# Block 1 of x through ACT's queue, the second gate weights moved ahead of blocks 2 and 3, and blocks 6 and 7 transposed by DMA

## The chip, the cores and the metric

The kernel runs on one core of a Trainium2 chip. The metric is the device time of one execution in microseconds (us); lower is better. The engines are named as in the profile: PE (TensorE, matmuls; PEld are its weight loads), DVE (VectorE), ACT (ScalarE), POOL (GpSimd) and SP (SyncE, which only issues DMAs here). PEq, ACTq and SPq are their instruction sequencers.

## The reference

The input x has 2048 tokens of 512 values. It is normalized, and two branches of the normalized x are added to x: a sliding-window attention (32 heads of 16, window 256) and a gated MLP whose gate is mixed over the tokens by a 2048 x 2048 matrix.

```python
xn = _layernorm(x)                                   # 2048 x 512
# branch A
q, k, v = split_heads(xn @ wqkv)                     # 32 heads of 16
p = softmax(where(0 <= i - j < 256, q @ k.T / 4, -1e9))
a = (p @ v) @ wo
# branch B
z = gelu(xn @ w_in)                                  # 2048 x 1376
z1, z2 = z[:, :688], _layernorm(z[:, 688:])
g = w_sp @ z2 + b_sp[:, None]                        # over the tokens
b = (z1 * g) @ w_out
out = x + a + b
```

All inputs and the output are bfloat16.

## The kernel before

The 2048 tokens are 16 blocks of 128 rows. The program is scheduled by hand: every engine runs its instructions in the order in which the code emits them, and a queue of DMAs goes out in the order of its issue.

The first stage (to about 54 us) makes the normalized and transposed x, called `xnT` (features on the partitions), and the two halves of z for each block. For a block n it consists of these steps:

- `load_x(n2)` (L189) loads blocks 2 n2 and 2 n2 + 1 into a tile `xs` by one DMA of 256 KB on SP's queue. With `split=True`, used for blocks 0 and 1 alone, it issues one DMA of 128 KB for each block (L194).
- `load_win(half, c0, c1)` (L203) loads two of the four row chunks of half of `w_in`, 344 KB. Half 1 gives z2 (the gate), half 0 gives z1.
- `stats(n)` (L252) computes mean and variance on DVE (L254, L255, L119) and the reciprocal root on POOL (L120).
- `norm(n)` (L258) normalizes on DVE (L260) into a tile `xn`. For n >= `X_DMA` (8) a DMA transpose on SP's queue then writes `xnT` (L265). For the others the tile is kept for `transpose_x(n)` (L269): four transposes on PE into PSUM (L274) and a copy by ACT (L277).
- `do_z(n, half)` (L279) runs eight matmuls on PE, four chunks by two column ranges (L285), and a GELU on ACT (L293).
- `z2_stats` and `z2_norm` normalize z2 on DVE (L298 to L304).

The order of DMAs on SP at the start is: block 0, block 1, gate weights chunks 0 and 1, blocks 2 and 3, gate weights chunks 2 and 3, blocks 4 and 5, the two parts of half 0 of `w_in`, blocks 6 and 7, `wqkv` (1536 KB), blocks 8 to 15, `wo`, and two pieces of `w_out`. Two one-element memsets on DVE hold some of them back: L313 (after the statistics of block 0) the half 0 of `w_in`, and L326 (after the statistics of block 3) `wqkv` and with it everything behind it on SP. After these come the DMA transposes of blocks 8 to 15 and of the first two rows of blocks of `w_sp` (`load_wsp`).

On PE the order is: 9 warm-up matmuls, transposes of block 0, 3 more warm-up matmuls, transposes of block 1, the gate half of blocks 0 and 1, transposes of block 2, half 0 of block 0, and then a loop over n from 2, whose body is

```python
            if n + 1 < X_DMA:
                transpose_x(n + 1)
            if n < NB:
                do_z(n, 1)
            if n + 3 < NB:
                stats(n + 3)
            if n + 2 < NB:
                norm(n + 2)
```

followed by `z2_stats(n - 2)`, the z2 norms, one of nine early projections of q, k or v once n >= 5 (`proj`, L129), and `do_z(n - 1, 0)`. ACT begins with the load of its function table and a warm-up activation (L216). A POOL instruction that forms a mask (L222) waits for this.

The second stage works through the list `ORDER`: scores, exponentials on ACT (L491), masks, values, the mixing of z2 with `w_sp` (L402) and the output (L433, L439, L444).

Of the kernel before, what the change touches and what calls it, by code (L numbers as in the profile page):

```python
# [8 lines left out]
P = 128  # L9
# [19 lines left out]
Z_RANGES = [(0, 512), (512, FH)]  # L29
NRING = 6  # L30
EBUFS = 7
X_DMA = 8
LAST = 128
ONB = 4
N_WARM = (9, 3)
# [33 lines left out]
def kernel(  # L69
# [12 lines left out]
    nc = tc.nc  # L82
    x2 = A_x.flatten_outer_dims()
# [94 lines left out]
    with tc.tile_pool(name="win_pool", bufs=1) as winp, tc.tile_pool(  # L178
# [10 lines left out]
        def load_x(n2, split=False):  # L189
            xs = xsp.tile([P, 2, D], BF, name="xs")  # L190
            if split:
                for j in range(2):
                    r = (2 * n2 + j) * P
                    nc.sync.dma_start(out=xs[:, j, :], in_=x2[r : r + P, :])  # L194
            else:
                nc.sync.dma_start(  # L196
                    out=xs[:],
                    in_=x2[2 * n2 * P : (2 * n2 + 2) * P, :].rearrange("(j p) d -> p j d", p=P),
                )
            for j in range(2):  # L200
                xs_tiles[2 * n2 + j] = xs[:, j, :]

        def load_win(half, c0, c1):  # L203
            nc.sync.dma_start(
                out=w_in_sb[:, c0:c1, half * FH : (half + 1) * FH],
                in_=B_w_in[c0 * P : c1 * P, half * FH : (half + 1) * FH].rearrange(
                    "(c p) f -> p c f", p=P
                ),
            )

        load_x(0, split=True)
        load_win(1, 0, 2)
        load_x(1)
        load_win(1, 2, 4)
        warm = sml.tile([P, 1], F32, name="warm")
        nc.scalar.activation(out=warm[:], in_=esel[:, 0:1], func=ACT.Gelu_apprx_tanh)  # L216

# [1 line left out]
            out=fmask[:], in_=fmask[:], pattern=[[-1, P]], compare_op=ALU.is_gt,  # L219
# [3 lines left out]
            out=esel[:], in_=esel[:], pattern=[[-32, 4]], compare_op=ALU.is_ge,  # L223
# [3 lines left out]
            out=esel[:], in_=esel[:], pattern=[[32, 4]], compare_op=ALU.is_ge,  # L227
# [30 lines left out]
        def norm(n):  # L258
# [4 lines left out]
            )  # L263
            if n >= X_DMA:
                nc.sync.dma_start_transpose(out=xnT[:, :, n * P : (n + 1) * P], in_=xn[:])  # L265
# [3 lines left out]
        def transpose_x(n):  # L269
            xn = xn_tiles.pop(n)  # L270
            pool, tag = (ps_y, "y") if n == 1 else (ps_g, "g")
            tp = pool.tile([P, NDC, P], BF, name="tp", tag=tag)
            for c in range(NDC):
                nc.tensor.transpose(  # L274
                    out=tp[:, c, :], in_=xn[:, c * P : (c + 1) * P], identity=ident[:]
                )
            nc.scalar.copy(out=xnT[:, :, n * P : (n + 1) * P], in_=tp[:])  # L277
# [34 lines left out]
        stats(0)  # L312
        nc.vector.memset(w_in_sb[0:1, 0, 0:1], 0.0)  # L313
        load_x(2)
        load_win(0, 0, 2)
        load_win(0, 2, 4)
# [12 lines left out]
        for n2 in range(4, NB // 2):  # L329
# [3 lines left out]
            out=w_out_sb[:, 0:5, :], in_=B_w_out[0:640, :].rearrange("(c p) n -> p c n", p=P)  # L333
# [9 lines left out]
            out=emask[:, 0:1], in_=esel[:], op=ALU.add, axis=mybir.AxisListType.X  # L343
        )
        nc.vector.tensor_scalar(
            out=emask[:, 1:2], in0=emask[:, 0:1], scalar1=-1.0, scalar2=1.0,
# [3 lines left out]
        for n in range(2, NB + 1):  # L350
            if n + 1 < X_DMA:
                transpose_x(n + 1)
# [220 lines left out]
    for i, t in enumerate(tokens):  # L573
        if i == last_proj + 1:
            for n in range(NB):
                xres[n] = xnT[:, n % NDC, (n // NDC) * D : (n // NDC + 1) * D]
            for c in range(NDC):
                nc.sync.dma_start(
                    out=xnT[:, c, :].rearrange("p (m d) -> p m d", d=D),
                    in_=x2.rearrange("(m c p) d -> c p m d", p=P, c=NDC)[c],  # L580
# [46 lines left out]
```

## Time and profile before

| | |
|---|---|
| median of 3 runs | 268.03 us (267.9 to 268.32) |
| the profiled execution's own time | 268.1 us |
| its span, first to last instruction | 266.1 us |
| TensorE clock granted | 1.0 throughout |
| PE busy | 258.6 us |
| ACT busy | 206.0 us |
| DVE busy | 197.3 us |
| POOL busy | 123.6 us |
| DMA | 23.63 MB, mean 89 GB/s |

The page has the busy time of each engine, a chain of waits followed back from the last instruction, and the costliest groups of instructions. The trace behind it can be asked for the order in time of a stretch (timeline: start, length, engine, line, operation; in brackets the idle time of the engine before it and what ended that), for the pieces of the chain in order of time, for the DMAs (KB of each and the us from issue to landing, a median where there are several) and for the busy time of each engine in given stretches. All times are from the start of the span. A DMA's time to landing holds its wait behind DMAs issued before it. The chain counts a pipelined matmul from the end of the one before it, so a piece of it can begin up to 0.2 us after the instruction's own start in the timeline.

### The profile page before, as it was taken

Reading aid. Unit: us, or ns where it says so; the run is one execution under the profiler, and the core shown is the slowest. Engines: PE = TensorE matmul, PEld = TensorE weight load, DVE = VectorE, ACT = ScalarE, POOL = GpSimd, SP = SyncE. Lnnn points to the kernel's source line nnn. Section 1 sums busy time; section 2 is a strip of 40 time slices with the busy share of each in tenths; the row PEclk is TensorE's granted clock in tenths of the full one; section 3 lists DMA queues with packets and bytes.
Section 4 is the critical chain, followed back from the end, with each engine's and each line's share of the span. In section 5 each row is a group of like instructions: output and inputs, shape, how many; then the busy total and the mean of one; then the engine's idle time right before and its main releaser. Section 6 shows DMA issues by size and latency. Waiting matters only on the chain.

```text
span 266.1 us, 8418 instructions
## 1 busy us (share of the span) xinstructions
PE 258.6 (97%) x3661; PEld 147.1 (55%) x3694; DVE 197.3 (74%) x384; ACT 206.0 (77%) x235; POOL 123.6 (46%) x140
## 2 busy tenths in 40 slices
PE   7999999999999999999999999999999999999995
PEld 2565665645455547554656656655665454554543
DVE  5999999567766778968788888767777658568542
ACT  3677767699999999999999899897899789553000
POOL 4334454115645256746637493156573617247200
PEclk9999999999999999999999999999999999999999
DMA  6992325700504050251312054033059972423733
GB/s 204 350 363 55 61 40 112 88 2 2 110 15 98 2 111 21 63 46 38 81 31 52 17 66 81 2 81 83 15 130 272 143 123 59 98 74 30 150 91 89
DMA packets 60132, 23.63 MB, mean 89 GB/s; under 512 B 51216, under 2 KB 59584, under 8 KB 60096
## 3 DMA queue, kind: packets, MB, share of 16 engines
q1 hardware_dynamic: 59472, 22.70, 38.5%
q8 instruction: 29, 0.48, 0.7%
q10 hardware_dynamic: 576, 0.39, 0.5%
q0 software_dynamic: 48, 0.00, 0.3%
q14 instruction: 7, 0.06, 0.1%
HBM read 8.41 MB, written 2.10 MB: 39 GB/s over the span
## 4 chain that ended last, share of the span: by engine, by line
PE 88%; ACT 7%; DMA 2%; issue 1%; SPq 1%; DVE 0%; ACTq 0%
PE gf L402 28%; PE zs L285 14%; PE S L483 11%; PE m L151 8%; PE o_t L531 8%; PE fo L439 8%; ACT E L491 7%; PE m L135 5%; PE fo L433 5%; DMA w_in_sb<-in_B_w_in_dram 2%; PE tp L274 1%; ACT L491 0%; DVE xnT L444 0%; SPq L194 0%; SPq L196 0%
## 5 line engine op out<-in xcount | busy, mean ns | idle before, releaser
L491 ACT ACTIVATE E<-S 128x1024 bf16<-128x1024 f32 x180 | 168.4, 1056 | 18.1 <-PE S L483 14.1
L402 PE MATMUL gf<-z_all,wspT 128*128 128x344 bf16 x512 | 94.2, 310 | 0.0
L502 POOL TENSOR_SCALAR_AFFINE_SELECT E<-E 128x1024 bf16<-128x1024 bf16 x64 | 79.3, 1264 | 18.1 <-ACT E L491 18.0
L402 PEld LDWEIGHTS <-wspT 128*128 128x128 bf16 x512 | 44.2, 98 | 33.8 <-issue 10.5
L554 POOL TENSOR_TENSOR o_norm<-o_c,rsum 128x256 bf16<-128x256 f32 x32 | 23.2, 726 | 77.3 <-DVE rsum L552 77.3
L507 DVE TENSOR_TENSOR E<-E,fmask 128x1024 bf16<-128x1024 bf16 x56 | 51.9, 954 | 1.6 <-ACT E L491 1.5
L285 PE MATMUL zs<-w_in_sb,xnT 128*128 128x176 bf16 (+1 forms) x250 | 39.7, 307 | 0.7 <-DMA w_in_sb<-in_B_w_in_dram 0.4
L483 PE MATMUL S<-q,k 32*128 32x128 bf16 (+2 forms) x888 | 38.5, 251 | 0.8 <-ACT E L491 0.8
L293 ACT ACTIVATE z_all<-zs 128x688 bf16<-128x688 f32 x32 | 23.8, 744 | 12.5 <-PE zs L285 12.5
L151 PE MATMUL m<-xnT,wqkv 128*128 128x512 bf16 x110 | 31.3, 379 | 0.9
L285 PEld LDWEIGHTS <-xnT 128*128 128x128 bf16 x256 | 22.2, 98 | 15.3 <-issue 0.6
L409 DVE SCALAR_TENSOR_TENSOR z_all<-gf,b_all,z_all 128x344 bf16<-128x344 f32 x32 | 18.2, 570 | 15.8 <-PE gf L402 15.7
L483 PEld LDWEIGHTS <-k 32*128 32x128 bf16 x888 | 15.2, 92 | 25.7 <-issue 23.7
L548 DVE STREAM_TRANSPOSE o_c<-o_t 128x512 f32<-128x512 f32 x32 | 22.3, 698 | 8.2 <-PE o_t L531 8.0
L531 PE MATMUL o_t<-E,v 128*32 128x128 bf16 x1440 | 24.5, 220 | 0.0
L531 PEld LDWEIGHTS <-v 128*32 128x32 bf16 x1440 | 20.3, 97 | 6.2 <-issue 6.0
L439 PE MATMUL fo<-w_out_sb,uT 128*128 128x512 bf16 (+2 forms) x98 | 23.0, 366 | 0.3 <-issue 0.2
L444 DVE TENSOR_TENSOR xnT<-fo,xnT 128x512 bf16<-128x512 f32 (+2 forms) x17 | 11.1, 657 | 13.6 <-PE fo L439 13.6
L171 DVE TENSOR_TENSOR k<-m,emask 128x1024 bf16<-128x1024 f32 x13 | 15.8, 1219 | 6.3 <-PE m L151 6.3
L151 PEld LDWEIGHTS <-wqkv 128*128 128x128 bf16 x128 | 12.0, 98 | 11.3 <-issue 0.9
L120 POOL TENSOR_TENSOR rstdx<-rs_v,negh 128x1 f32<-128x1 f32 x16 | 10.3, 646 | 16.1 <-DVE rs_v L119 14.7
L298 DVE BATCH_NORM_STATS2 st<-z_all 128x6 f32<-128x344 bf16 x32 | 14.9, 506 | 3.7 <-ACT z_all L293 3.7
(51 smaller groups left out, 177.4 us busy)
## 6 DMA issues: line engine op xcount, KB each, us to landing
xnT<-in_A_x_dram SPq DMA_DIRECT2D x4, 512.0 KB, 6.4
xs<-in_A_x_dram SPq DMA_DIRECT2D x7, 256.0 KB, 7.5
out_dram<-xnT SPq DMA_DIRECT2D x13, 128.0 KB, 1.7
wqkv<-in_A_wqkv_dram SPq DMA_DIRECT2D x1, 1536.0 KB, 7.2
w_in_sb<-in_B_w_in_dram SPq DMA_DIRECT2D x4, 344.0 KB, 5.1
w_out_sb<-in_B_w_out_dram SPq DMA_DIRECT2D x1, 640.0 KB, 10.4
wo_sb<-in_A_wo_dram SPq DMA_DIRECT2D x1, 512.0 KB, 9.1
xs<-in_A_x_dram SPq DMA_DIRECT2D x2, 128.0 KB, 2.1
```

What stands on the lines that cost most here:

```text
L151: nc.tensor.matmul(m, lhsT=wqkv[:, c, w0 : w0 + P], rhs=xnT[:, c, grp * 512 : (grp + 1) * 512], start=(c == 0), stop=(c == NDC - 1),)
L285: nc.tensor.matmul(zp[:, lo:hi], lhsT=xnT[:, c, n * P : (n + 1) * P], rhs=w_in_sb[:, c, f0 + lo : f0 + hi], start=(c == 0), stop=(c == NDC ...
L293: nc.scalar.activation(out=dst[:, n, 0:FH], in_=zp[:, 0:FH], func=ACT.Gelu_apprx_tanh)
L402: nc.tensor.matmul(gf[:, 0:FQ], lhsT=wsp_tiles[n][:, c, :], rhs=z2_all[:, c, lo : lo + FQ], start=(c == 0), stop=(c == NB - 1),)
L439: nc.tensor.matmul(fo[:, c0:c1], lhsT=uT_tiles[n][:, c, :], rhs=w_out_sb[:, c, c0:c1], start=False, stop=(c == NFC - 1),)
L483: nc.tensor.matmul(S[:, h2, j * P : (j + w) * P], lhsT=k_t[(G, kb // 4)][32 * s : 32 * s + 32, e, (kb % 4) * P : (kb % 4 + 1) * P], rhs=q_ ...
L491: nc.scalar.activation(out=E[:, j : j + 3 : 2, 0:nb, :].rearrange("p h b c -> p h (b c)"), in_=tiles[pr][:, :, 0 : nb * P], func=ACT.Exp, ...
L502: nc.gpsimd.affine_select(out=E[:, :, j, :], in_=E[:, :, j, :], pattern=[[0, 8], [1, P]], compare_op=ALU.is_ge, fill=0.0, base=0, channel_ ...
L507: nc.vector.tensor_tensor(out=E[:, :, j, :], in0=E[:, :, j, :], in1=fmask[:].unsqueeze(1).to_broadcast([P, 8, P]), op=ALU.mult,)
L531: nc.tensor.matmul(T[32 * s : 32 * s + 32, e, j * P : (j + 1) * P], lhsT=v_t[(G, kb // 4)][:, kb % 4, s, e : e + 2, :].rearrange("p a d -> ...
L548: nc.vector.transpose(out=C[:, 0 : 32 * DH], in_=Tb)
L554: nc.gpsimd.tensor_tensor(out=o_n[:], in0=c_o.rearrange("p e q d -> p q e d"), in1=rsum[:].rearrange("p e q -> p q e").unsqueeze(3).to_bro ...
```

## The change

Three edits. `X_DMA` goes from 8 to 6, so that blocks 6 and 7 are transposed by DMA on SP's queue instead of by PE and ACT. Block 1 is loaded by a DMA that ACT issues, as its first instruction, ahead of its table load. And the DMA of chunks 2 and 3 of the gate weights is issued ahead of the one of blocks 2 and 3.

```diff
-X_DMA = 8
+X_DMA = 6
...
             if split:
                 for j in range(2):
                     r = (2 * n2 + j) * P
-                    nc.sync.dma_start(out=xs[:, j, :], in_=x2[r : r + P, :])
+                    (nc.sync, nc.scalar)[j].dma_start(out=xs[:, j, :], in_=x2[r : r + P, :])
...
         load_x(0, split=True)
         load_win(1, 0, 2)
+        load_win(1, 2, 4)
         load_x(1)
-        load_win(1, 2, 4)
```

The order of the instructions on each engine is otherwise the same. PE has 16 rows less (eight transposes and their weight loads), ACT two copies less and one DMA more, SP one load less and two transposes more.

## The prediction

> **What bounds the kernel now.** I read the page first, for the engine that fills the span, then the chain of waits over the first 56 us, because every edit acts before 25 us, then the timeline of that stretch, and last the transfers one by one. From the page:
>
> ```profile
> PE 258.6 (97%) x3661; PEld 147.1 (55%) x3694; DVE 197.3 (74%) x384; ACT 206.0 (77%) x235; POOL 123.6 (46%) x140
> PE 88%; ACT 7%; DMA 2%; issue 1%; SPq 1%; DVE 0%; ACTq 0%
> ```
>
> TensorE is busy for 97% of the span and is 88% of the chain. So a microsecond that TensorE gains or loses early reaches the end whole, unless another engine sets the pace in between. The only such stretch of note is 56.0 to 71.8 us (17 exponentials of ACT on the chain); it starts when the last GELU of the first stage ends at 53.97, so it moves with TensorE. The first stage's own chain, rows of start, length and what:
>
> ```profile
> 2.71 4.97 DMA w_in_sb<-in_B_w_in_dram
> 7.72 1.91 PE zs L285 x12
> 9.63 0.22 PE tp L274 x4
> 22.19 0.22 PE tp L274 x4
> 22.41 1.17 PE zs L285 x8
> ```
>
> The chain waits for one transfer, the second half of the gate weights, until 7.68; after that it is TensorE alone, and a group of four transposes costs it 0.22. The timeline shows what stands just behind:
>
> ```profile
> 6.17 0.69 DVE L254 BATCH_NORM_STATS2 st<-xs 128x6 f32<-128x512 bf16 x1
> 7.72 1.91 PE L285 MATMUL zs<-w_in_sb,xnT 128*128 128x512 bf16 x12 [0.43 <-DMA w_in_sb<-in_B_w_in_dram]
> 8.19 0.41 DVE L260 TENSOR_SCALAR xn<-xs,mvx,rstdx 128x512 bf16<-128x512 bf16 x1
> 8.31 0.37 SPq L328 DMA_DIRECT2D wqkv<-in_A_wqkv_dram  x1
> 16.15 0.41 DVE L260 TENSOR_SCALAR xn<-xs,mvx,rstdx 128x512 bf16<-128x512 bf16 x1
> 22.35 6.95 SPq L265 DMA_TRANSPOSE xnT<-xn  x3
> ```
>
> These are the statistics of block 2 (6.17), its normalization (8.19), the issue of wqkv, the normalization of block 6 (16.15), and the first transposes that go by DMA. Two things matter. DVE has no idle time marked from 6.17 to beyond 40 us, so what makes block 2 late makes all its later work late. And the first DMA transpose is issued at 22.35, when the transfers have just run dry: the last of the loads (the 48 KB tail of w_out, issued at 13.58) takes 8.9 us and lands at 22.5.
>
> ```profile
> w_out_sb<-in_B_w_out_dram SPq DMA_DIRECT2D x1, 48.0 KB, 8.9
> xnT<-xn SPq DMA_TRANSPOSE x8, 2.4
> wspT<-in_B_w_sp_dram SPq DMA_TRANSPOSE x1, 9.8
> wspT<-in_B_w_sp_dram SPq DMA_TRANSPOSE x1, 4.4
> ```
>
> The last two rows are the same transpose twice: issued at 200.28 behind four 512 KB loads, and issued at 191.08 with nothing ahead. It takes 9.8 instead of 4.4, so a transpose waits its turn behind loads already queued.
>
> **Block 1 through ACT.** SP issues one DMA less: 0.41 and the 0.05 behind it, so all later issues up to the next gate come 0.46 earlier. Block 1 itself landed at 3.45 and DVE takes it at 3.97: 0.5 of cover. Block 0 now shares the DMA engines with it; the two landed 0.53 apart, so block 0 is at most 0.5 later, and that is hidden behind the wait for block 2 below (z of blocks 0 and 1 would then end at 9.4 instead of 8.9, before 9.7). ACT issues the DMA ahead of its table load; its own later issues take 0.33 to 0.39. Behind it are the warm-up activation, a POOL select that waits for that, and POOL's first reciprocal root, before which POOL idles 0.85. So 0.4 is covered; without cover it would cost 0.4. [...]
>
> **Second gate weights ahead of blocks 2 and 3.** Before, 856 KB were queued up to blocks 2 and 3 (landed 5.9) and 1200 KB up to the second weights (7.68). Now the weights are at 944 KB: 5.9 + 88/344 x 1.78 = 6.4, less 0.46 is 5.9. TensorE needs them after its first four matmuls, at 6.55 + 0.58 = 7.13. So the wait of 0.59 goes, and blocks 0 and 1 (16 matmuls at 0.146) end at 8.89. What is late next is block 2: blocks 2 and 3 now stand at 1200 KB and land at 7.68 - 0.46 = 7.2 (bounds 6.5, if the rings keep even pace, and 7.7, if nothing comes earlier). From the start of block 2's statistics to the end of its normalization DVE takes 8.60 - 6.17 = 2.43. So it ends at 9.65, the transposes start 0.06 later (5.38 to 5.44 for block 0), at 9.71 instead of 9.47. TensorE, in order, idles 0.8 at that point: the wait has changed its cause, and the net is +0.24 (bounds -0.48 and +0.72). DVE runs 1.05 late from there. Normalizations of blocks 4 and 5 have 1.9 and 2.1 of slack against their transposes and stay covered; block 3's ends at 10.98 against transposes wanted at 11.1 to 11.2, just covered.
>
> The memset that gates wqkv (L326) stands behind block 3's statistics on DVE and slides from 8.20 to 9.25. Behind it on SP are wqkv, blocks 8 to 15, wo and w_out: 3.7 MB that TensorE needs late (wqkv lands at 15.5, first used at 20.0).
>
> **Blocks 6 and 7 by DMA.** Removed: eight transposes, 2 x 0.22 on the chain; two ACT copies of 0.58, where ACT is idle part of the time, nothing. Added: two DMA transposes, 1.19 of SP time each, and no TensorE work. Block 6's row is normalized by 16.56 + 1.05 = 17.6. TensorE used to start its z at 22.25; with 0.44 gone and 0.24 lost it would start at 22.05. By the unloaded 2.4 the transpose would land at 20.0, in time. But the queue holds the loads until the w_out tail. The landing is 22.5 + s + t.
>
> s, the later loads: the gate slides by 1.05 and the bounds are 0 and 1.1. The slowest rings still held block 6 and 7's x until 11.0; wqkv issued at 9.36 has data flowing 1.2 later (a lone DMA transpose issued at 22.35 shows its first traffic in the slice from 23.5), at 10.6, and the earlier loads end at 11.0 - 0.46 = 10.5. So the slow rings lose next to nothing: I take 0.1, nearest to that row.
>
> t, the transpose behind loads: a uT transpose right behind a wspT transpose landed 0.8 after it. The wspT transpose behind the four loads landed at 210.1, 3.4 after the last of them (issued 199.59, 7.1), which saves 1.0 on its unloaded 4.4; the same saving on 2.4 gives 1.4. Bounds 0.7 and 1.5; I take 0.9, the uT row being closest in size.
>
> So block 6 lands at 23.5, its first matmul starts at 23.56 instead of 22.25: **+1.3 us**. That swallows the +0.24 (the wait is shorter by it). Block 7 lands about 0.8 behind, 24.3, and is wanted 3.3 after block 6, at 26.9: free. Blocks 8 to 15 landed 4 us before use: free, with DVE 1.05 late. [...]
>
> **Sum.** 268.1 (span 266.1 and 2.0 around it) + 1.3 = 269.4 for the profiled execution, which lies 0.07 above the median: 269.3.
>
> **Rivals.**
> - The transposes arrive in time (not slower). If block 6 lands before 22.05, only +0.24 - 0.44 = -0.2 is left: 267.8. For it: the loads' bulk is done by 20.5 (275 GB/s in 20.0 to 20.5, 104 and 51 after it), only a few rings work on to 22. Against: a transpose needs every ring, and it decides only if the slowest ring ends 1.4 earlier. Chance 0.15.
> - The same, and blocks 2 and 3 land at 6.5: -0.48 - 0.44 = -0.9, 267.1: both the wait and the transposes are saved. For it: the weights before them landed at 6.5 on most rings, if the slow ones had kept pace. Against: those rings were late in the execution shown. Chance 0.08.
> - The gate's slide passes whole (s = 1.1): block 6 lands at 24.5, +2.3, 270.3. For it: the transfers run at 340 to 410 GB/s from 10.5 to 20, so a late start is not made up. Against: a dip to 198 and 186 GB/s stands there already. Chance 0.18.
> - A transpose behind loads starts only when they have all landed: 22.6 + 2.4 = 25.0, +2.8, 270.8. For it: the wspT one was 6.23 in SP's issue and SP was free only as the last load landed. Against: it saved 1.0. Chance 0.09.
>
> **How the numbers follow.** The forecast gets 0.50. About 0.2% (0.54 us) is what a measurement here can tell from no change. Faster: the 267.1 case and a little of the first rival, 0.09. Same: the rest of that rival and the lower edge of the forecast (t = 0.5 with s below 0), 0.18. Slower: 0.73. The range runs from 267.4, below the in-time case, to 271.0, past the late cases; what it leaves out is most of the fastest case and the far edge of the last.
>
> **What would show it.** In the profile after: no wait for gate weights at 7.7; instead TensorE waits 0.5 to 1 us for block 2's normalization near 9.7; DVE's block 2 statistics start near 7.2; wqkv is issued near 9.4; the w_out tail lands near 22.6; block 6's DMA transpose, issued near 17.7, takes over 5 us; and TensorE idles some 1.5 us before block 6's z, waiting for that DMA. If that DMA lands before 22 us, or TensorE's wait there is gone, I am wrong; if it waits 3 us, the late rivals hold.

## The result, and the profile after

The changed kernel takes 272.54 us (median of 6 runs, 271.11 to 273.12) against 268.26 us beside it: a ratio of 1.0152, 95% interval 1.0126 to 1.0178. It is slower, as forecast, but by 4.3 us instead of 1.3, and outside the range that was given. Two executions further down, of 274.91 us (blocks 6 and 7 by DMA alone) and 277.61 us (the changed kernel again), lie over 1.5% above the fastest of their kernel, are put down to a slower state of the machine, and are left out of medians and ratios.

The profiled execution is the shortest of the six: 271.11 us, span 269.1, so its trace explains 3.0 of the 4.3. The page's lines of busy time and of the chain, after:

```profile
PE 262.0 (97%) x3686; PEld 147.6 (55%) x3686; DVE 197.0 (73%) x384; ACT 205.1 (76%) x233; POOL 123.7 (46%) x140
PE 82%; ACT 7%; DMA 5%; DVE 4%; issue 1%; SPq 0%; ACTq 0%
```

6% of the chain went from PE to DMA and DVE. TensorE has eight transposes less and is busy longer, but by less than the 3.4 us between the two pages: the trace before lacks the records of 33 of its 3694 matmuls, and three runs below that have all of them, with the transposes of before, are busy for 260.2 to 260.9. The chain's pieces in order of time show where (start, length, what; of a row of DVE pieces only the first is copied):

```profile
2.26 5.17 DMA xs<-in_A_x_dram
7.46 0.71 DVE st L254
...
17.89 7.36 DMA xnT<-xn
25.25 0.05 issue
25.30 1.34 PE zs L285 x8
```

Before, the chain waited for weights until 7.68 and was TensorE's own from there. Now it waits for the x of blocks 2 and 3 (landed 7.43), runs on DVE until block 6 is normalized, and then sits 7.36 us in block 6's transpose. That z begins at 25.30; before, its first matmul began at 22.25 (last of the next three rows, from the timeline before). The difference, 3.05, is the 3.0 of the span. From there on the order of work is the same.

```profile
5.44 0.40 PE L274 MATMUL tp<-ident,xn 128*128 128x128 bf16 x4 [0.17 <-DVE xn L260]
5.67 0.81 PE L246 MATMUL warm_t<-zeros 128*128 128x512 bf16 x3
22.25 0.96 PE L285 MATMUL zs<-w_in_sb,xnT 128*128 128x512 bf16 x5
```

The timeline of the same stretch after the change:

```profile
3.59 0.69 DVE L254 BATCH_NORM_STATS2 st<-xs 128x6 f32<-128x512 bf16 x1 [2.24 <-DMA xs<-in_A_x_dram]
6.09 0.61 PE L274 MATMUL tp<-ident,xn 128*128 128x128 bf16 x4 [0.81 <-DVE xn L260]
6.49 1.49 PE L246 MATMUL warm_t<-zeros 128*128 128x512 bf16 x3
8.20 3.42 PE L285 MATMUL zs<-w_in_sb,xnT 128*128 128x512 bf16 x16
9.61 0.37 SPq L328 DMA_DIRECT2D wqkv<-in_A_wqkv_dram  x1
25.30 1.34 PE L285 MATMUL zs<-w_in_sb,xnT 128*128 128x512 bf16 x8 [1.35 <-DMA xnT<-xn]
```

Of the first four rows only the later block 0 was foreseen. It is taken at 3.59 instead of 2.95, TensorE pauses 0.81 before its transposes (0.17 before), and the three warm-up matmuls behind them take 1.49 (0.81 before). The sixteen matmuls of blocks 0 and 1 take 3.42; at 0.146 each on the chain of before it would be 2.3. That is TensorE at half clock, until about 10: up to 9.8 the matmul behind one of 512 columns starts 0.43 after it, from 10.28 on 0.21. The page's clock row doesn't show it, because the first clock record of this trace only starts at 10.06. Before, it starts at 5.16, so the 1.0 of that profile does not speak for the nine warm-up matmuls ahead of it either (4.02 us, 0.45 each; 0.43 from one start to the next, where the three behind 5.16 have 0.21). Both traces change pace within 0.6 us of where their first record starts, so in the other traces too that start is read as the rise of the clock. The last row is TensorE's wait for block 6's DMA. The transfers themselves, w_out's tail (issued 14.06) and block 6's transpose (issued 17.89), us to landing in the last column:

```profile
w_out_sb<-in_B_w_out_dram SPq DMA_DIRECT2D x1, 48.0 KB, 11.0
xnT<-xn SPq DMA_TRANSPOSE x1, 7.4
```

The tail lands at 25.0, 2.5 later than before, and the transpose 0.2 behind it. Both sizes differ in other traces of the same edits; the part on why the prediction was wrong has them side by side.

### The profile page after: what moved, and what is told of

It reads as the page before. It is cut to its first block, busy times and chain, and to the rows that moved or that the text cites. A ratio compares the mean times of both kernels' runs of the same rounds, so it can differ in the third digit from the quotient of the medians.

```text
span 269.1 us, 8438 instructions
## 1 busy us (share of the span) xinstructions
PE 262.0 (97%) x3686; PEld 147.6 (55%) x3686; DVE 197.0 (73%) x384; ACT 205.1 (76%) x233; POOL 123.7 (46%) x140
## 4 chain that ended last, share of the span: by engine, by line
PE 82%; ACT 7%; DMA 5%; DVE 4%; issue 1%; SPq 0%; ACTq 0%
PE gf L402 28%; PE S L483 11%; PE zs L285 9%; PE m L151 8%; PE o_t L531 8%; PE fo L439 8%; ACT E L491 7%; PE fo L433 5%; PE m L135 5%; DMA xnT<-xn 3%; DMA xs<-in_A_x_dram 2%; DVE st L254 1%; DVE st L298 1%; DVE xn L260 1%; ACT L491 0%
## 5 line engine op out<-in xcount | busy, mean ns | idle before, releaser
L491 ACT ACTIVATE E<-S 128x1024 bf16<-128x1024 f32 x180 | 168.4, 1055 | 18.1 <-PE S L483 14.1
L285 PE MATMUL zs<-w_in_sb,xnT 128*128 128x512 bf16 (+1 forms) x256 | 40.7, 314 | 1.3 <-DMA xnT<-xn 1.3
L151 PE MATMUL m<-xnT,wqkv 128*128 128x512 bf16 x128 | 32.6, 379 | 0.0
L439 PE MATMUL fo<-w_out_sb,uT 128*128 128x512 bf16 (+2 forms) x102 | 23.5, 367 | 0.0
```

The costliest lines, as they stand in the source:

```text
L151: nc.tensor.matmul(m, lhsT=wqkv[:, c, w0 : w0 + P], rhs=xnT[:, c, grp * 512 : (grp + 1) * 512], start=(c == 0), stop=(c == NDC - 1),)
L285: nc.tensor.matmul(zp[:, lo:hi], lhsT=xnT[:, c, n * P : (n + 1) * P], rhs=w_in_sb[:, c, f0 + lo : f0 + hi], start=(c == 0), stop=(c == NDC ...
L439: nc.tensor.matmul(fo[:, c0:c1], lhsT=uT_tiles[n][:, c, :], rhs=w_out_sb[:, c, c0:c1], start=False, stop=(c == NFC - 1),)
L491: nc.scalar.activation(out=E[:, j : j + 3 : 2, 0:nb, :].rearrange("p h b c -> p h (b c)"), in_=tiles[pr][:, :, 0 : nb * P], func=ACT.Exp, ...
```

## The experiments

Two theories stood after the result. Queue: block 6's transpose waits for the loads ahead of it in SP's queue. Clock: TensorE's pauses lower its clock, so that a pause costs again after it has ended. The first four runs did the parts of the change alone.

**Block 1 through ACT alone.**

```diff
-                    nc.sync.dma_start(out=xs[:, j, :], in_=x2[r : r + P, :])
+                    (nc.sync, nc.scalar)[j].dma_start(out=xs[:, j, :], in_=x2[r : r + P, :])
```

> Block 1 through ACT alone. Queue theory (the loss is block 6's DMA transpose waiting behind the loads): nothing is lost here, 268.1 us within 0.4. Clock theory (block 0 shares the DMA engines, lands 0.65 later, TensorE pauses before block 0's transposes and its clock rises only near 10 us): block 0's statistics start near 3.6, the three matmuls before block 1's transposes take 1.49 us instead of 0.81, blocks 0 and 1 end near 11.4, and the time is up by 1.5 to 2 us, about 269.8.

Measured: 268.45 us against 268.13, ratio 1.0021 (0.9998 to 1.0044). The executions differ: eight lie between 267.86 and 268.68, one at 269.04, and three between 270.05 and 270.41. The queue theory holds for the median. An excess of 2 us, the size that the clock theory gave, shows in three of twelve; the kept trace (269.04) is none of them. In it the clock rose at 4.56, ahead of a pause of 1.17, and the warm-up matmuls behind the pause took 0.81.

**Second gate weights ahead alone.**

```diff
         load_win(1, 0, 2)
+        load_win(1, 2, 4)
         load_x(1)
-        load_win(1, 2, 4)
```

> Second gate weights ahead of blocks 2 and 3 alone, all on SP. Queue theory: no more than a small change. Clock theory: none either, block 0 lands at 2.9 as before. Wait theory (the wait for the weights becomes a wait for block 2): no idle time at 7.3, blocks 2 and 3 land at 7.7, block 2's transposes start near 10.2 instead of 9.47, time +0.7, about 268.8; wqkv is issued near 9.8.

Measured: 268.27 us, ratio 1.0004 (0.999 to 1.0017). So there is no effect, and the wait theory's 0.7 is refuted. The pause at 7.3 is gone, blocks 2 and 3 landed at 6.7, not 7.7, and TensorE doesn't wait for block 2: its row is normalized at 9.15, its transposes start at 9.39 (9.47 before). That the trace gains nothing has another reason than a new wait. Its clock rose at 6.56 instead of 5.16, and the first transposes and the three warm-up matmuls took 0.61 and 1.19 instead of 0.40 and 0.81; about what the missing wait gave. What the edit would give with the early clock isn't shown.

**Blocks 6 and 7 by DMA alone.**

```diff
-X_DMA = 8
+X_DMA = 6
```

> Blocks 6 and 7 by DMA alone, loads as before. Queue theory: block 6's transpose is issued near 16.6, the w_out tail lands near 22.5, block 6 at 23 to 23.7, TensorE waits 1.2 to 1.9 us for it, time +1.0 to +1.5, about 269.3; and if the wait also lowers TensorE's clock for a while, up to 1.7 more. Clock theory (all of the loss is at the start): -0.4, about 267.6.

Measured: 271.45 us, ratio 1.0098 (1.0068 to 1.0127). This is most of the loss, and it shows both theories in one trace. First TensorE's timeline, then the busy time in stretches (stretch, length, then busy us and instructions of PE, PEld, DVE, ACT and POOL, the granted clock, the DMA share and GB/s):

```profile
24.05 1.85 PE L285 MATMUL zs<-w_in_sb,xnT 128*128 128x512 bf16 x8 [2.62 <-DMA xnT<-xn]
```

```profile
22.00:24.00 2.00, 0.00 (x0) 0.00 (x0) 1.97 (x7) 0.21 (x1) 1.00 (x3) 1.00 0.91 97
24.00:24.70 0.70, 0.65 (x5) 0.41 (x6) 0.70 (x2) 0.00 (x0) 0.00 (x0) 1.00 0.52 107
24.70:28.20 3.50, 3.50 (x13) 1.55 (x11) 3.29 (x13) 1.30 (x2) 1.93 (x4) 0.51 0.19 37
28.20:30.00 1.80, 1.80 (x13) 1.04 (x12) 1.77 (x6) 0.77 (x2) 0.61 (x2) 1.00 0.34 69
```

TensorE stands still for 2.62 us. It starts again at 24.05 at full clock, and from 24.7 to 28.2 the granted clock is 0.51: 13 matmuls in 3.5 us, where the next 1.8 us hold 13 as well. The record behind this is a stretch of 3.41 us at half clock from 24.74. Half of that, 1.7 us, is lost on top of the wait. Block 6's z begins 1.8 later than before (24.05 for 22.25), and 1.8 and 1.7 make 3.5, about the 3.4 that the span is longer. The granted clock doesn't explain every execution of this run: beside 271.53 and 271.76 at 0.994 and 269.74 at 1.0 there is one of 271.45 at 1.0.

**Both load edits, X_DMA still 8.**

```diff
-                    nc.sync.dma_start(out=xs[:, j, :], in_=x2[r : r + P, :])
+                    (nc.sync, nc.scalar)[j].dma_start(out=xs[:, j, :], in_=x2[r : r + P, :])
...
+        load_win(1, 2, 4)
         load_x(1)
-        load_win(1, 2, 4)
```

> Both load edits, X_DMA still 8. Queue theory: no loss beyond the wait for block 2, 268.1 to 268.6. Clock theory: TensorE is slow until 10 us as in the changed kernel, blocks 0 and 1 end near 11.45 instead of 9.63 and nothing hides it, +1.8 to +2.0, about 270.

Measured: 268.7 us, ratio 1.0025 (1.0004 to 1.0046), ten executions between 268.15 and 269.17, two at 270.24 and 271.1. As with the first: little, and about 2 us in a few executions. The clock theory's figure of 270 for all of them was wrong. The loads do slide: the tail of w_out lands at 24.1 in this run, 1.6 later than before.

The next four runs took the suspected causes away.

**Blocks 6 and 7 by DMA, with wo and w_out behind block 7's transpose.**

```diff
-        nc.sync.dma_start(out=wo_sb[:], ...)       # and the two pieces of w_out
...
             if n + 2 < NB:
                 norm(n + 2)
+            if n == 5:
+                nc.sync.dma_start(out=wo_sb[:], ...)   # and the two pieces of w_out
```

> Blocks 6 and 7 by DMA alone, but wo and w_out (1200 KB) issued behind block 7's transpose instead of ahead of block 6's. Queue theory: ahead of block 6 are only blocks 8 to 15 and wqkv, which land by 17.5 to 19.3, so block 6 lands near 19.5, TensorE does not wait at 21.4 and its clock stays up: 267.6 (268.1 less the 0.44 of two transpose groups). Theory that a DMA transpose itself is slow beside other traffic: still late, 269 or more.

Measured: 267.51 us against 268.04, ratio 0.999 (0.9976 to 1.0003). The same transpose, with wqkv and blocks 8 to 15 ahead of it but not wo and w_out, takes 2.9 us from issue to landing instead of 7.4 (first line: dma67_only, second: this run):

```profile
xnT<-xn SPq DMA_TRANSPOSE x1, 7.4
xnT<-xn SPq DMA_TRANSPOSE x1, 2.9
```

TensorE does not wait for it. The transposes by DMA are not slow here; their place in the queue was.

**All three edits, with wo and w_out behind block 7's transpose.** Against the changed kernel:

```diff
-        nc.sync.dma_start(out=wo_sb[:], ...)       # and the two pieces of w_out
...
+            if n == 5:
+                nc.sync.dma_start(out=wo_sb[:], ...)   # and the two pieces of w_out
```

> All three edits, with wo and w_out issued behind block 7's transpose. Queue theory: the two load edits cost what they cost alone (0.2 to 0.6), less 0.44: 268.0 to 268.4. If it stays above 270, the loss is not in the queue ahead of block 6.

Measured: 268.41 us, ratio 1.0023 (1.0008 to 1.0038), where the changed kernel was 1.0152. The three load DMAs in another place take away 3.9 of the 4.3 us between the medians. Block 8's transpose now waits behind them (5.0 us to landing), and TensorE stops 0.27 us for it. Two of the twelve executions are near 270, and the kept trace is one of them: its last two stores of the output took 3.6 and 3.3 us to land (1.6 and 1.5 before), behind the last matmul. So not every extra 2 us comes from the first stage.

**Blocks 6 and 7 by DMA, the wait filled with matmuls.**

```diff
+            if n == 6:
+                warm_up(9)
             if n < NB:
                 do_z(n, 1)
```

> Blocks 6 and 7 by DMA alone, and nine warm-up matmuls (1.95 us at full clock, result unused) just ahead of block 6's z, inside the wait for its transpose. Clock theory (the wait costs twice, once as idle time and once as 3.4 us at half clock behind it): no half-clock stretch, 269.7 to 270, 1.7 less than blocks 6 and 7 by DMA without them. Queue theory without the clock: no change, 271.5.

Measured: 270.31 us, ratio 1.0082 (1.0062 to 1.0101). In its trace the fillers run from 21.82 to 23.92 and the clock stays at 1.0:

```profile
21.82 2.10 PE L246 MATMUL warm_t<-zeros 128*128 128x512 bf16 x9
23.76 1.33 PE L285 MATMUL zs<-w_in_sb,xnT 128*128 128x512 bf16 x8
```

The medians differ by 1.1 (271.45 and 270.31), and the two intervals overlap, so the times alone don't settle the size of the clock's part. The two traces do. The second stage's first exponential starts at 59.51 with the transposes alone and at 57.52 with fillers (first two rows):

```profile
59.51 1.02 ACT L491 ACTIVATE E<-S 128x1024 bf16<-128x1024 f32 x1
57.52 1.94 ACT L493 ACTIVATE E<-S 128x1024 bf16<-128x1024 f32 x2
44.06 14.33 DMA b_bf<-in_B_b_sp_dram
```

Of these 1.99 us, 0.29 stand already at block 6's z (24.05 and 23.76); the other 1.70 are the slow clock. The traced execution with fillers then loses 1.50 again, on something else: TensorE waits at 57.7 for work behind the 4 KB load of `b_sp` (third row, of the chain), which took 14.3 us to land where it took 6.1 before.

**Block 7 alone by DMA.**

```diff
-X_DMA = 8
+X_DMA = 7
```

> Block 7 alone by DMA, all else as before. Queue theory: block 7's transpose is issued near 19.7, lands near 23.5 to 24, and is wanted at 25.3: no wait, 267.9 (268.1 less 0.22). A cost for any transpose by DMA in this stretch would show as half of what two of them cost, 269.5.

Measured: 267.87 us, ratio 0.9989 (0.9979 to 0.9999). Block 7's transpose takes 3.1 us and lands at 22.9, before its z. So it is block 6's transpose that made the loss, not block 7's.

The last four runs were on the size of the clock's part, and on a better version.

**The changed kernel again, and with six fillers ahead of block 6's z.** The first has no edit, the second, against the changed kernel:

```diff
+            if n == 6:
+                warm_up(6)
             if n < NB:
                 do_z(n, 1)
```

> The changed kernel once more, beside the others of this set. Queue and clock theory together: executions with a granted clock of 1.0 near 271, those with 0.994 (one stretch of 3.4 us at half clock behind the wait for block 6) near 272.5; median 272. If the executions at 0.994 are no longer than those at 1.0, the clock costs nothing.

> The changed kernel with six warm-up matmuls (1.3 us at full clock, result unused) ahead of block 6's z, inside the wait for its transpose. Clock theory: no execution at 0.994, all near 271, 1.3 less than the changed kernel. Queue theory alone: no change or up to 0.3 more.

Measured: 271.88 us, ratio 1.0141 (1.0117 to 1.0164), and with fillers 270.87 us, ratio 1.0097 (1.008 to 1.0114). The intervals are just apart, and the ratios differ by 1.2 us: that much of the loss goes with the fillers. The executions say the same. Of both runs of the changed kernel, those with a granted clock of 1.0 took 270.73, 271.11 and 271.27, those with 0.994 took 271.88 to 273.12. With fillers all six had 1.0 and took 269.92 to 271.02. 0.6% of 270 us is 1.6 us, what one stretch of 3.4 at half clock takes.

**Block 1 through ACT, with eleven instead of nine warm-up matmuls at the start.**

```diff
-N_WARM = (9, 3)
+N_WARM = (11, 3)
```

> Block 1 through ACT alone, with eleven instead of nine warm-up matmuls at the start, so that TensorE is busy until about 6.1, when the late block 0 is ready. Clock theory (the executions near 270 in the run with this edit alone come from TensorE's pause of about 1 us there, which in some executions leaves its clock at half until 10 us): no execution above 269.3, median 268.1 to 268.4. Otherwise again some executions near 270.

Measured: 268.14 us against 267.87, ratio 1.0003 (0.9994 to 1.0012), eleven executions between 267.83 and 268.41. None is near 270, and in the trace TensorE no longer pauses ahead of block 0's transposes. This fits the clock theory. It doesn't prove it: with three such executions in twelve, eleven without one would still come by chance about one time in 24 (0.75 to the eleventh power is 0.04), and no trace of one near 270 was kept.

**The better version: blocks 6 and 7 by DMA, wo and w_out behind the last transpose of x.**

```diff
-X_DMA = 8
+X_DMA = 6
...
-        nc.sync.dma_start(out=wo_sb[:], ...)       # and the two pieces of w_out
...
+        nc.sync.dma_start(out=wo_sb[:], ...)   # after the loop, and the two pieces of w_out
         z2_stats(NB - 1)
```

> Blocks 6 and 7 by DMA, block 1 and the gate weights as before, and wo and w_out issued behind the last DMA transpose of x, near 43. Queue theory: block 6 lands near 19.9, blocks 8 to 15 as before, no wait for any of them: 267.5, 0.5 below the kernel before. If wo and w_out now make the transposes of w_sp late, TensorE waits for those after 54 and the gain is gone: 268 or more.

Measured: 267.31 us against 267.87, ratio 0.9973 (0.9962 to 0.9985): 0.3% faster than the kernel before, about what the two transpose groups cost it (0.44 on its chain). Its page, which lacks 32 matmul records:

```profile
PE 258.5 (97%) x3654; PEld 146.7 (55%) x3686; DVE 197.4 (74%) x384; ACT 205.0 (77%) x233; POOL 123.6 (47%) x140
PE 87%; ACT 7%; DMA 3%; issue 1%; DVE 1%; SPq 0%; ACTq 0%
```

## Why the prediction was wrong

The wait that was forecast is the one that came: block 6's transpose waits behind the loads, and TensorE waits for it. Taking wo and w_out out of the way removed 3.9 of the 4.3 us. What failed is the size of one term and a term that wasn't in the sum. For the terms s and t the traces have to be read side by side. The gate here is the memset of L326 that holds wqkv back; all times in us:

| run | wqkv issued | w_out's tail landed | block 6 landed |
|---|---|---|---|
| before | 8.31 | 22.49 | |
| weights ahead alone | 8.86 | 23.15 | |
| block 1 through ACT alone | 9.04 | 23.36 | |
| both load edits | 9.92 | 24.11 | |
| blocks 6 and 7 by DMA alone | 8.37 | 23.80 | 24.01 |
| the same with fillers | 8.24 | 22.29 | 23.40 |
| the change | 9.61 | 25.03 | 25.25 |
| the change, again | 10.00 | 24.34 | 25.47 |
| the change with fillers | 9.49 | 23.84 | 24.93 |

- **s, the later loads, 0.1 forecast, 1.3 measured: the step that failed.** The prediction let the gate slide by 1.05 and took nearly all of it as absorbed, because slow rings would still hold older data (in the trace before, every load and transpose lands in 16 parts; of the x of blocks 6 and 7, 14 were in by 10.44, the last two at 10.99 and 11.01). The first four rows have none of the two new transposes, and in them the tail follows wqkv's issue by 14.2 to 14.3 us each time: a slide of 0.55, 0.73 and 1.61 makes it 0.7, 0.9 and 1.6 later. The slide passes whole. In the changed kernel it is 1.3 (9.61 for 8.31).
- **t, what comes on top, 0.9 forecast, 1.0 to 1.5 measured.** Block 6's landing less 22.49 and less the slide of its row is 1.5, 1.0, 1.5, 1.3 and 1.3 in the last five rows. The forecast was a little low; its own bounds were 0.7 and 1.5. The t of 0.5 that is named with the chance of no change is shown by no run; the lowest measured is 1.0. So the landing in the profile after is 22.5 + 1.3 + 1.5 = 25.3, where 23.5 was forecast. In three of these rows the tail lands in step with wqkv (14.1 to 14.4 after it) and the transpose 1.1 behind it. In the other two, the profile after among them, the tail itself is about 1.2 late and the transpose lands 0.2 behind it. What makes the tail late in these two is open.
- **The clock behind the wait, not in the sum, 1.2 to 1.4 measured.** 1.2 is what the fillers take away; 1.4 lies between the medians of the executions at 1.0 (271.11) and at 0.994 (272.55, 8 of the 11 compared). The prediction took a wait as costing its own length. This is the difference between the trace's 3.0 and the median's 4.3. Without it the changed kernel would take about 271.1, at the very edge of the range.

The other steps:

- Block 1 through ACT: "at most 0.5 later, hidden" was wrong by a little in size and in kind. Block 0 landed 0.65 later, and TensorE's clock stayed at half until 10, so that blocks 0 and 1 ended at 11.45, not at 8.9 or 9.4. That the pause of 0.81 did this is inferred: in both kept traces of the changed kernel the clock rises behind the pause, at 10.06 and 9.87; in three other traces it had risen ahead of a pause of 0.82, 1.11 or 1.17 (at 4.91, 3.99 and 4.56), and there the three warm-up matmuls behind the pause took 0.81. In the changed kernel the slow start is hidden in the wait for block 6, where TensorE then stands 1.35 instead of the 2.62 with the transposes alone. Alone, the edit's ratio is 1.0021, with an interval that holds 1.
- The wait for block 6, "some 1.5", measured 1.35: right by luck. The transpose landed 1.75 later than forecast, and TensorE, slow at the start, came to it 1.9 later.
- Weights ahead: that TensorE now waits for block 2 is right where the clock rose early and both load edits stand (0.68 with both load edits, 0.41 in the change with fillers). In the profile after there is no such wait, because TensorE itself was late. Block 2's statistics start at 7.46 (7.2 forecast), wqkv is issued at 9.61 (9.4). The edit alone measured as nothing.
- Two transpose groups saved 0.44: right; 0.56 between the medians in the better version.
- Block 7 free: right. Blocks 8 to 15 free: right.
- Of the rivals, "the gate's slide passes whole" held. "Starts only when all have landed" did not: the transpose landed 0.2 to 1.1 behind the last load, not 2.4. Its 25.0 for the landing is close by chance. Each rival was priced without the clock, and with the clock the time lies above the range.

That the executions of the changed kernel at 0.994 have their slow stretch just behind the wait for block 6 is inferred from the trace with the transposes alone and from the fillers; no trace of such an execution of the changed kernel was kept. Why three of eleven lack it is open too. Both kept traces at 1.0 have the slow start, so TensorE comes late to block 6 and waits only 1.35 and 1.59; an execution with a fast start would come earlier and wait longer. This is a reading, not a measurement.

## What to carry to other kernels

A DMA that an engine needs soon should not be issued behind loads that nobody needs soon: in all five traces with that order it landed 0.2 to 1.1 us behind the last of them, and the loads' order is free to change. When a load's gate or place is moved, follow it to the last transfer behind it in the queue, not to the first. A long wait of TensorE can cost twice, once as the wait and once as the slow clock behind it: here one of 2.62 us did (1.7 on top), and those of 1.35 and 1.59 did not. Matmuls whose result isn't used, put into the wait, took the second cost away (1.70 us between two traces; 1.1 and 1.2 between the runs). And before one trace's split of a delay is taken as the rule, look at a second trace of the same queue.

## What the runs showed of the hardware that was not expected

**The clock fell behind a pause that was shorter than the slow stretch.** The trace with the transposes alone has clock records of 20.48 us at 1.0, 3.41 at 0.5 and 242.35 at 1.0: 6, 1 and 71 times 3.41. In the 3.41 us before the slow stretch, 21.33 to 24.74, TensorE was busy for about 0.8, the pause being 2.62; pauses of 1.35 and 1.59 us in the two kept traces of the changed kernel lowered nothing. What decides between them no run shows.

**A transpose behind loads landed sooner after them than one alone took.** Alone, a transpose of a block took 2.4 us from issue to landing (the median of the eight in the kernel before). Queued behind loads, block 6's landed 0.2 to 1.1 us behind the last of them, and block 7's 0.5 to 0.7 behind block 6's (25.25 and 25.73 in the changed kernel). Whether queued transposes hold up the loads ahead of them stays open: w_out's tail was about 1.2 late in two of the five traces with both transposes queued, and on time in the other three, which include a second trace of the same changed kernel.
